# Cosine attention followed by a highway layer: half-batch loads and norms, a power on GpSimd, first quads turned on TensorE, a new planned order

## The chip, the cores and the metric

The kernel runs on one core of a Trainium2 chip. The metric is the time of one execution on the device in microseconds (us); smaller is better. Before the change two executions took 439.52 and 444.78 us, a median of 442.15 us. The profiled execution has a span of 442.0 us; all times inside the kernel below are from that one.

## The reference

There are 8 batches, 12 heads, 448 positions and a head size of 64. Queries and keys are divided by their own norms, the scores are scaled by 1/tau = 10, and a softmax over the keys weighs the values. The heads are then put side by side to rows of 768, and a highway layer is applied to the 3584 rows.

```python
q_n = q / (np.linalg.norm(q, axis=-1, keepdims=True) + 1e-06)
k_n = k / (np.linalg.norm(k, axis=-1, keepdims=True) + 1e-06)
scores = np.matmul(q_n, k_n.transpose(0, 1, 3, 2)) / tau
attn = np.exp(scores - np.max(scores, axis=-1, keepdims=True))
attn = attn / (np.sum(attn, axis=-1, keepdims=True) + 1e-09)
x = np.matmul(attn, v)                    # then (batch, position, head x 64)
H = np.maximum(x @ w_h, 0.0)
T = 1.0 / (1.0 + np.exp(-(x @ w_t + b_t)))
out = T * H + (1.0 - T) * x
```

Since normalised rows have scores of at most 10 in size, both kernels leave out the subtraction of the maximum.

## The kernel before

**Units of work.** Four heads of one batch are a *quad* (24 in all, three a batch), two heads are a *pair* (48), and 128 rows of the highway layer are a *tile* (28). A batch gives three tiles of its own, and the 64 positions that are left over in each batch are joined for two batches into a fourth tile (`xl`), so two batches make seven tiles.

**A quad on its way.** GpSimd (POOL) issues the loads of queries and keys (L260), which turn fp32 into fp16 on the way, into one of five `raw` buffers. VectorE (DVE) squares them (L275), folds the squares twice (L282, L289) and sums them (L294). When the three quads of a batch are there, eight small VectorE operations on 84 values a partition (`newton`, L307 to L313) give the inverse norms `rs`; in batch 0 this is done for each quad by itself. GpSimd multiplies queries and keys with them into one of two `qkn` buffers (L361, L365, L369; 15 rows a quad, since one row of the queries is kept twice). Two DMA transposes issued by SyncE (L387) then turn `qkn` into one of three `qkT` buffers. VectorE copies the values into `vp` with a further column for the sum of the weights (L397, L398, L399).

**A pair on its way.** TensorE (PE) makes the scores in four steps (L422, L425), ScalarE (ACT) takes the exponential of each step (L438, L440), PE multiplies with the values in 32 small matmuls (L463), and VectorE divides by the sum (L471, L473, L477) into `xb` and, for the left-over positions, `st`.

**A tile on its way.** When the six pairs of a batch are done, SyncE moves the left-over rows (L496) and turns the three blocks of `xb` (L514) into `xT`. PE multiplies each with both weights, in two halves each (L525; the bias is one more matmul, L528). VectorE takes relu minus x (L539), ScalarE the tanh (L546), VectorE adds 1 to it, multiplies and makes the last sum (L557, L558, L559), and SyncE stores the rows (L575). The kernel carries x/2 in place of x (the value of the sum column is 2), so that the tanh needs no scale.

**What sets the order.** All of this is a list of operations with an engine, a cost in ns, a due step, the operations it depends on, and the buffers that it takes and drops. `Planner.plan` runs the list once at build time: each engine takes, of the operations that are ready by the planned times, the one with the lowest due step. The result is written out as a fixed order for each engine. On the chip every engine works through its own order and waits at an operation whose inputs or buffers are not there, however much work stands ready behind it. The planner's costs are therefore no times of the chip, but they decide which operation stands before which. PSUM has three shared banks (`pb`) for the attention result and the halves of the highway layer, two double banks for the scores and one bank for their last step.

Of the kernel before, what the change touches and what calls it, by code (L numbers as in the profile page):

```python
# [7 lines left out]

# [6 lines left out]


class Op:
    __slots__ = ("eng", "dur", "fn", "deps", "step", "takes", "drops", "mode",
                 "land", "start", "end", "left", "users", "seq", "name", "after", "issued")

    def __init__(self, name, eng, dur, step, fn, deps=(), takes=(), drops=(), mode=None, land=None, after=()):
        self.name, self.eng, self.dur, self.step, self.fn = name, eng, dur, step, fn
        self.deps = [d for d in deps if d is not None]
        self.takes, self.drops, self.mode, self.land = list(takes), list(drops), mode, land
        self.start = self.end = None
        self.users = []
        self.after = [d for d in after if d is not None]


class Ring:  # L30


    def __init__(self, bufs):
        self.free = list(range(len(bufs)))
        self.bufs = bufs
        self.where = {}
        self.users = {}
# [5 lines left out]
class Planner:  # L43


    SYNC = 90
    SWITCH = 93
    DMA_FIX = 1900
    GBPS = 300.0
# [4 lines left out]
    def add(self, *a, **k):  # L54
        op = Op(*a, **k)
        op.seq = len(self.ops)
        self.ops.append(op)
        return op

    def plan(self):  # L60
        ready = {e: [] for e in ("PE", "ACT", "DVE", "POOL", "SP")}
# [4 lines left out]
        for op in self.ops:  # L66
            if op.left == 0:
                ready[op.eng].append((0.0, op))
        free = {e: 0.0 for e in ready}
        dma_free = 0.0  # L70
        mode = None
        now = 0.0
        pend = []
        order = []
        n = len(self.ops)
        while len(order) < n:
# [8 lines left out]
            for e in ready:  # L85
# [3 lines left out]
                for t, op in ready[e]:  # L89
                    if t > now:  # L90
                        continue
                    need = {}
# [4 lines left out]
                    key = op.step  # L97
                    if e == "PE" and mode is not None and op.mode == mode and mode == "q":
# [6 lines left out]
                ready[e].remove((t, op))  # L105
                for ring, key in op.takes:
                    ring.where[key] = ring.free.pop(0)
                dur = op.dur
# [5 lines left out]
                free[e] = op.issued = now + dur  # L114
                end = now + dur
                if op.land is not None:
                    begin = max(end, dma_free)
                    dma_free = begin + op.land / self.GBPS
                    end = dma_free + self.DMA_FIX
                op.end = end  # L120
                for ring, key in op.drops:
                    pend.append((end + self.SYNC, ring, ring.where[key]))
                for u in op.users:
                    u.left -= 1
                    if u.left == 0:
                        r = max([d.end + (self.SYNC if (d.eng != u.eng or d.land is not None) else 0) for d in u.deps]
                                + [d.issued for d in u.after])
                        ready[u.eng].append((r, u))
# [6 lines left out]
            nxt += [t for t, _, _ in pend if t > now]  # L135
            if not nxt:
# [3 lines left out]
        self.span = max(o.end for o in self.ops)  # L140
        return order


@with_exitstack
def kernel(
# [20 lines left out]
    pool = ctx.enter_context(tc.tile_pool(name="sb", bufs=1))  # L166
    psum = ctx.enter_context(tc.tile_pool(name="ps", bufs=1, space=bass.MemoryType.PSUM))

    def ring(name, n, shape, dt, space=None):
        return Ring([(space or pool).tile(shape, dt, name=f"{name}{i}", tag=f"{name}{i}") for i in range(n)])  # L170

    w_sb = [pool.tile([128, CC, DM], FP16, name=n, tag=n) for n in ("w_h", "w_t")]
    brow = pool.tile([128, DM], FP16, name="brow", tag="brow")
    ones = pool.tile([128, 128], FP16, name="ones", tag="ones")
    braw = pool.tile([1, DM], FP32, name="braw", tag="braw")

    raw_r = ring("raw", 5, [128, 2, 2, 7, D], FP16)
    sq_r = ring("sq", 2, [128, 28, D], FP16)
# [446 lines left out]
```

## Time and profile before

| What | us | Share of the 442.0 us |
|---|---|---|
| PE busy | 273.3 | 62% |
| DVE busy | 258.7 | 59% |
| ACT busy | 170.1 | 38% |
| POOL busy | 147.0 | 33% |
| DMA: q1, what SyncE issued, of 16 engines | | 51.6% |
| DMA: q0, what GpSimd issued, of 16 engines | | 21.1% |
| Mean granted TensorE clock | | 0.837 of full |

A group of instructions is named by its line, its engine and what it writes and reads (out<-in). A wait is time in which an engine stood still, put down to whatever released it last. "SPq" is the queue of SyncE, on which DMAs are issued. Busy times of PE are those of pipelined matmuls, so two matmuls that overlap count once. In a timeline, the first number is the start, the second how long the row lasted; "x6" is a row of six instructions merged.

Two rows of the page give the prices that matter most here: an exponential of 896 elements takes 921 ns (L438, 144 times, 126.2 us in all), and a product of 448 elements on GpSimd takes 992 ns in the mean (L365, 48 times, 46.5 us).

### The profile page before, as it was taken

The page shows a single profiled execution, that of the slowest core. Times are in us where ns is not written, and L with a number is a line of the kernel's source. Part 1 is how long each engine was busy: PE and PEld are TensorE (multiplying, and loading weights), DVE is VectorE, ACT ScalarE, POOL GpSimd, SP SyncE. Part 2 cuts the span into 40 slices and gives each one's busy share as a digit, 9 for nine tenths or more (in the row PEclk, how much of TensorE's full clock was granted, in tenths as well). Part 3 has the DMA queues.
Part 4 walks back from the last instruction along what each step waited for, and adds up shares of the span by engine and source line. Part 5 has one row for each costly group of instructions (what it writes and reads, how often), then busy time and mean ns, then how long its engine had stood idle before and what let it go on. Part 6 is the DMA issues. An engine that isn't in the chain of part 4 may idle for free.

```text
span 442.0 us, 6960 instructions
## 1 busy us (share of the span) xinstructions
PE 273.3 (62%) x2648; PEld 149.6 (34%) x2648; DVE 258.7 (59%) x556; ACT 170.1 (38%) x249; POOL 147.0 (33%) x207
## 2 busy tenths in 40 slices
PE   0014382768519595298509596496709696698494
PEld 0003151343304353154304344243405344255252
DVE  2893254285915859159914868549823968365154
ACT  1022361336405263066504373073704373178021
POOL 5657005620366005650176005460085005430000
PEclk9999556796959889599957988799958988899798
DMA  8699932996099930999179951999269941872413
GB/s 171 106 186 188 180 52 48 180 162 148 2 162 177 190 78 25 186 207 177 36 109 171 200 75 38 149 204 199 59 84 184 172 117 36 153 116 55 99 42 101
DMA packets 111234, 55.50 MB, mean 126 GB/s; under 512 B 81505, under 2 KB 107617, under 8 KB 111202
## 3 DMA queue, kind: packets, MB, share of 16 engines
q1 hardware_dynamic: 96578, 41.70, 51.6%
q0 software_dynamic: 14624, 13.37, 21.1%
q8 instruction: 20, 0.33, 0.3%
q14 instruction: 12, 0.10, 0.1%
HBM read 39.32 MB, written 11.01 MB: 114 GB/s over the span
## 4 chain that ended last, share of the span: by engine, by line
DMA 31%; PE 25%; DVE 20%; POOL 9%; SPq 7%; issue 5%; ACT 2%; POOLq 0%; DVEq 0%; ACTq 0%
DMA qkT<-qkn 24%; PE pb L525 16%; DMA xT<-xb 5%; PE pb L463 4%; PE sc L422 4%; POOL qkn L365 3%; POOL raw L260 3%; DVE xb L473 3%; SPq L387 2%; SPq L514 2%; SPq L496 2%; DVE sq L275 2%; POOL qkn L369 2%; DVE o L559 1%; DMA out_dram<-o 1%
## 5 line engine op out<-in xcount | busy, mean ns | idle before, releaser
L438 ACT ACTIVATE ex<-sc 128x896 f16<-128x896 f32 x144 | 126.2, 921 | 109.7 <-PE sc L422 109.5
L525 PE MATMUL pb<-w_h,xT 128*128 128x384 f16 x336 | 80.1, 393 | 81.0 <-DMA xT<-xb 74.4
L525 PEld LDWEIGHTS <-xT 128*128 128x128 f16 x672 | 68.3, 109 | 152.2 <-DMA xT<-xb 75.9
L361 POOL TENSOR_TENSOR qkn<-raw,rs 128x128 f16<-128x128 f16 x48 | 20.2, 439 | 242.8 <-DVE rd L471 183.8
L422 PE MATMUL sc<-qkT 64*128 64x448 f16 x288 | 51.2, 397 | 65.3 <-DMA qkT<-qkn 60.2
L546 ACT ACTIVATE t<-pb 128x384 f16<-128x384 f32 x56 | 27.7, 494 | 155.8 <-PE pb L528 155.6
L525 PE MATMUL pb<-w_t,xT 128*128 128x384 f16 x336 | 70.9, 352 | 3.6 <-DVE d L539 3.0
L463 PE MATMUL pb<-vp,ex 128*128 128x65 f16 x1536 | 64.0, 200 | 12.6 <-DVE st L477 6.5
L463 PEld LDWEIGHTS <-ex 128*128 128x128 f16 x1536 | 58.8, 102 | 24.8 <-issue 14.7
L539 DVE SCALAR_TENSOR_TENSOR d<-pb,xb 128x384 f16<-128x384 f32 x48 | 25.3, 551 | 67.8 <-PE pb L525 67.8
L365 POOL TENSOR_TENSOR qkn<-raw,rs 128x448 f16<-128x448 f16 x48 | 46.5, 992 | 0.2
L369 POOL TENSOR_TENSOR qkn<-raw,rs 128x384 f16<-128x384 f16 x48 | 44.2, 940 | 0.0
L422 PEld LDWEIGHTS <-qkT 64*128 64x128 f16 x288 | 11.9, 96 | 91.2 <-DMA qkT<-qkn 62.5
L557 DVE TENSOR_SCALAR t<-t 128x768 f16<-128x768 f16 x28 | 18.7, 669 | 37.1 <-ACT t L546 37.0
L471 DVE RECIPROCAL rd<-pb 128x7 f32<-128x7 f32 x48 | 9.7, 201 | 47.3 <-PE pb L463 47.0
L275 DVE TENSOR_TENSOR sq<-raw 128x1792 f16<-128x1792 f16 x24 | 26.0, 1084 | 6.7 <-DMA raw<-in_k_dram 6.5
L473 DVE TENSOR_TENSOR xb<-pb,rd 128x384 f16<-128x384 f32 x48 | 26.7, 557 | 1.6
L440 ACT ACTIVATE ex<-sl 128x448 f16<-128x448 f32 x48 | 26.4, 550 | 0.0
L559 DVE SCALAR_TENSOR_TENSOR o<-xb,d 128x768 f32<-128x768 f16 x24 | 24.6, 1026 | 0.8
L558 DVE TENSOR_TENSOR d<-t,d 128x768 f16<-128x768 f16 x28 | 23.8, 849 | 1.0
L425 PE MATMUL sl<-qkT 64*64 64x448 f16 x96 | 19.9, 411 | 0.0
L528 PE MATMUL pb<-brow,ones 128*128 128x384 f16 x56 | 18.6, 332 | 0.0
(37 smaller groups left out, 169.9 us busy)
## 6 DMA issues: line engine op xcount, KB each, us to landing
out_dram<-o SPq DMA_DIRECT2D x48, 192.0 KB, 2.8
vraw<-in_v_dram SPq DMA_DIRECT2D x8, 768.0 KB, 9.6
raw<-in_q_dram POOLq DMA_DIRECT2D x24, 224.0 KB, 9.2
raw<-in_k_dram POOLq DMA_DIRECT2D x24, 224.0 KB, 9.8
vraw<-in_v_dram SPq DMA_DIRECT2D x8, 576.0 KB, 6.6
vraw<-in_v_dram SPq DMA_DIRECT2D x8, 192.0 KB, 10.9
out_dram<-o SPq DMA_DIRECT2D x4, 384.0 KB, 3.2
w_h<-in_moe_w_h_dram POOLq DMA_DIRECT2D x1, 1152.0 KB, 10.7
```

Of the source, the lines that this page charges most:

```text
L275: nc.vector.tensor_mul(sq_r[k_][:, :, :], r, r)
L365: nc.gpsimd.tensor_mul(qkn[:, 1:8, g, :], raw[:, 0, g], rs[:, 0, g].unsqueeze(2).to_broadcast([128, 7, D]))
L369: nc.gpsimd.tensor_mul(qkn[:, 8:14, g, :].rearrange("p (j i) d -> p i j d", i=2), raw[:, 1, g, 0:6, :].rearrange("p (i j) d -> p i j d", i=2),
L422: nc.tensor.matmul(sc_r[n, j][:, g, 0:S], lhsT=T[:, 512 + 128 * j : 640 + 128 * j], rhs=rhs, start=True, stop=True)
L438: nc.scalar.activation(o, sc_r[n, j][:, :, 0:S], AF.Exp, scale=inv_tau)
L440: nc.scalar.activation(ex[:, 3136 : 3136 + S], sl_r[n][:, 0:S], AF.Exp, scale=inv_tau)
L463: nc.tensor.matmul(u[:, s * 65 : s * 65 + 65], lhsT=l, rhs=r, start=(m == 0), stop=(m == len(ms) - 1))
L473: nc.vector.tensor_tensor(out=xo, in0=u[:, 0:6, 0:D].rearrange("p (g i) e -> p g i e", g=2), in1=rd[:, 0:6].rearrange("p (g i) -> p g i", ...
L525: nc.tensor.matmul(pt[:, 0:MH], lhsT=xT[:, c, :], rhs=w_sb[w][:, c, ms], start=(c == 0), stop=(w == 0 and c == CC - 1))
L539: nc.vector.scalar_tensor_tensor(out=d_r[m][:, h], in0=pb_r[m, w, h][:, 0:MH], scalar=0.0, in1=xsrc()[:, ms], op0=ALU.max, op1=ALU.subtract)
L546: nc.scalar.activation(t_r[m][:, h], pb_r[m, w, h][:, 0:MH], AF.Tanh)
L559: nc.vector.scalar_tensor_tensor(out=o_r[m][:, :], in0=xsrc(), scalar=2.0, in1=d, op0=ALU.mult, op1=ALU.add)
```

## The change

The loads come in half batches, each into one of three `raw` buffers of a whole batch, batch 0 still in three parts. Squares, folds and sums work on the same halves. In batches 0 and 1 the inverse norms are still Newton steps, for each part; in the other six batches one GpSimd operation raises the 84 sums of squares to the power -0.5. `qkn` gets a third buffer, and its rows are 14 in place of 15. The first two quads (all of batch 0 but its last third) are not turned by DMA: their products are shared out between GpSimd and VectorE, PE turns them against an identity into PSUM, and ScalarE or VectorE copies them to `qkT`. The values are copied by ScalarE or VectorE and their last row is masked on GpSimd in one operation a batch; `vp` now holds a batch. x is carried whole: the tanh is scaled by 0.5, the gate is (t+1)/2, by VectorE or GpSimd, and the last sum, d + x, can be made by GpSimd too. The weights are loaded in halves. Many planner costs are new, an operation may be given to whichever of two engines is free first, and loads are planned only while the planned DMA backlog is small.

It is meant to have norms and transposes ready earlier, to lift small work off VectorE, and to start the first scores without waiting for DMA.

In the order that the new planner gives, 15 of the 28 last sums, 9 of the 28 gates and all 8 masked copies stand on GpSimd; 15 of the 24 copies of values and the 4 copies of turned quads on ScalarE; 10 of the 12 products of the first two quads on VectorE. On PE the finished batch's first tile comes after the scores and attention of the next batch's first one or two pairs, but for the boundary of batches 1 and 2; before, it came ahead of the next batch's scores at each boundary.

The core of the diff:

```diff
-    SYNC = 90
-    SWITCH = 93
-    DMA_FIX = 1900
-    GBPS = 300.0
+    SYNC = 70
+    SWITCH = 95
+    LATE = 1900
+    DEPTH = 2500
...
+                    if op.dma is not None and op.dma[1] == "load" and dma_free > now + self.DEPTH:
+                        continue
...
-    raw_r = ring("raw", 5, [128, 2, 2, 7, D], FP16)
...
-    qkn_r = ring("qkn", 2, [128, 15, 2, D], FP16)
...
+    raw_r = ring("raw", 3, [128, 2, 6, 7, D], FP16)
...
+    qkn_r = ring("qkn", 3, [128, 14, 2, D], FP16)
+    qkT_r = ring("qkT", 3, [128, 2, 14, 64], FP16)
...
+    vp_r = ring("vp", 2, [128, NH, 4, 66], FP16)
...
-    xb_r = ring("xb", 3, [128, 3, DM], FP16)
+    xb_r = ring("xb", 2, [128, 3, DM], FP16)
...
+        return lambda op: nc.gpsimd.dma_start(w_sb[i][:, 3 * h : 3 * h + 3, :], src[:, 3 * h : 3 * h + 3, :])
+
+    w_ops = {(i, h): add(f"w{i}{h}", ("POOL", 890), (-1.8, -1.6, -1.4, -1.2)[2 * i + h], w_load(i, h), dma=(3350, "load"))
+             for i in range(2) for h in range(2)}
...
+        return lambda op: nc.gpsimd.dma_start(raw_r[b][:, t, lo:hi], src[:, 6 * b + lo : 6 * b + hi, :])
...
-            lq = add(f"lq{k_}", "POOL", 1000, s0 - 9, mk_load(k_, 0), takes=[(raw_r, k_)], land=128 * 896 * 4,
-                     after=[qT_op.get((k_ - 3, 1))])
-            lk = add(f"lk{k_}", "POOL", 1000, s0 - 9, mk_load(k_, 1), after=[lq], land=128 * 896 * 4)
...
-            o = add(f"nw{b}", "DVE", 8 * 225, steps(b * NQ) - 4.5, newton(b, 0, 84), deps=[red_ops[b * NQ + 2]],
-                    takes=[(rs_r, b)], drops=[(n2_r, b)])
-            norm_ops[b] = [o, o, o]
...
+        parts = [(0, 2), (2, 4), (4, 6)] if b == 0 else [(0, 3), (3, 6)]
+        for lo, hi in parts:
+            for t in range(2):
+                o = add(f"l{'qk'[t]}{b}_{lo}", ("POOL", 730), 6 * b - 9 + lo * (0.3 if b == 1 else 1), mk_load(b, t, lo, hi),
+                        takes=[(raw_r, b)] if lo == 0 and t == 0 else [], dma=(700 * (hi - lo), "load"))
+                if not (lo == 0 and t == 0):
+                    o.after.append(ld[b, 0, 0])
+                for i in range(lo, hi):
...
+        def power(b):
+            def fn(op):
+                nc.gpsimd.tensor_tensor(out=rs_r[b][:, :, :], in0=n2_r[b][:, :, :],
+                                        in1=half[:, :].unsqueeze(2).to_broadcast([128, 2, 42]), op=ALU.pow)
+            return fn
+
+        groups = parts if b < 2 else [(0, 6)]
+        prev = None
+        for lo, hi in groups:
+            first, last = lo == 0, hi == 6
+            kw = dict(deps=[reds[parts.index((lo, hi))]] if b < 2 else reds, after=[prev],
+                      takes=[(rs_r, b)] if first else [], drops=[(n2_r, b)] if last else [])
+            if b < 2:
+                o = add(f"nw{b}_{lo}", ("DVE", 8 * (195 + 14 * (hi - lo) * 1.042)), 6 * b + lo - 4.5, newton(b, lo, hi), **kw)
+            else:
+                o = add(f"nw{b}_{lo}", ("POOL", 2500), 6 * b + lo - 4.5, power(b), **kw)
...
+        for w, n in enumerate((128, 64, 448, 384, 384, 384)):
+            engs = {"POOL": (pool(n), 0.0)}
+            if k_ < NPE:
+                engs["DVE"] = (dve(n), 0.0)
+            o = add(f"nm{k_}_{w}", engs, s0 - 3.5, nm_fn(k_, b, qd, w), deps=[rs_op[b, 2 * qd], rs_op[b, 2 * qd + 1]], after=nms[:1],
+                    takes=[(qkn_r, k_)] if w == 0 else [])
+            nms.append(o)
+        if lastq:
+            nms[-1].drops += [(raw_r, b), (rs_r, b)]
...
+        if k_ < NPE:
+            cps = []
+            for t in range(2):
+                def pt_fn(op, k_=k_, t=t):
+                    ps = pb_r["tr", k_, t][:, 0:448].bitcast(FP16)
+                    for s in range(7):
+                        nc.tensor.transpose(ps[:, 128 * s : 128 * s + 128],
+                                            qkn_r[k_][:, 7 * t + s].rearrange("p g d -> p (g d)"), ident[:, :])
+
+                need = nms[1:4] if t == 0 else [nms[0]] + nms[4:]
+                pt = add(f"pt{k_}_{t}", ("PE", 7 * 55), s0 - 2.5, pt_fn, deps=need + [i_id], takes=[(pb_r, ("tr", k_, t))],
+                         mode="f")
...
+                def cp_fn(op, k_=k_, t=t):
+                    ps = pb_r["tr", k_, t][:, 0:448].bitcast(FP16).rearrange("p (s a l) -> p s a l", s=7, a=2)
+                    dst = qkT_r[k_][:, :, 7 * t : 7 * t + 7, :].rearrange("p a s l -> p s a l")
+                    if op.eng == "ACT":
+                        nc.scalar.copy(dst, ps)
...
+                cp = add(f"cp{k_}_{t}", {"ACT": (act(896), 0.0), "DVE": (dve(896, 2), 0.0)}, s0 - 2.5, cp_fn, deps=[pt], after=cps,
+                         takes=[(qkT_r, k_)] if t == 0 else [], drops=[(pb_r, ("tr", k_, t))])
...
+            nc.gpsimd.tensor_mul(vp_r[b][:, :, 3, 0:D], vraw_r[b][:, :, 3, :], mask[:, :].unsqueeze(2).to_broadcast([128, NH, D]))
+
+        vlo = add(f"vl{b}", ("POOL", pool(768)), 6 * b - 1.5, vl_fn, deps=vl[b] + [ini_m] + ini_vp, takes=[(vp_r, b)])
+        prev = vlo
...
+            o = add(f"vc{b}_{qd}", {"ACT": (act(768), 0.0), "DVE": (dve(768, 2), 1.5)}, 6 * b + 2 * qd - 1.0, vc_fn,
+                    deps=vl[b], after=[prev], drops=[(vraw_r, b)] if qd == NQ - 1 else [])
...
+        def g_fn(op, m=m):
+            t = t_r[m][:, :, :].rearrange("p h m -> p (h m)")
+            eng = {"POOL": nc.gpsimd, "DVE": nc.vector}[op.eng]
+            eng.tensor_scalar(out=t, in0=t, scalar1=1.0, scalar2=0.5, op0=ALU.add, op1=ALU.mult)
...
-            nc.vector.tensor_scalar(out=t, in0=t, scalar1=1.0, scalar2=None, op0=ALU.add)
...
+        g1 = add(f"g{m}", {"DVE": (380, 0.0), "POOL": (900, 1.5)}, s0 + 1.8, g_fn, deps=el)
+        gg = add(f"h{m}", ("DVE", 590), s0 + 1.8, h_fn, deps=[g1], drops=[(t_r, m)])
...
+            eng.tensor_add(o_r[m][:, :], d, xsrc())
+
+        oo = add(f"o{m}", {"POOL": (pool(768), 0.0), "DVE": (dve(768), 1.5)}, s0 + 1.9, o_fn, deps=[gg], takes=[(o_r, m)],
...
-            nc.vector.scalar_tensor_tensor(out=o_r[m][:, :], in0=xsrc(), scalar=2.0, in1=d, op0=ALU.mult, op1=ALU.add)
```

## The prediction

> **What bounds the kernel now.** I read the page's slices first, then the waits in order of their total, then the timelines around one batch boundary, then the busy time by stretch. In the slices no engine is full for long:
>
> ```profile
> PE   0014382768519595298509596496709696698494
> POOL 5657005620366005650176005460085005430000
> DMA  8699932996099930999179951999269941872413
> ```
>
> One digit is 11 us. PE and the DMA engines alternate: DMA stands at 9 while PE is in the middle of its range and at 0 to 3 where PE is at 9, and POOL works in bursts with empty slices between. That is a chain that hands work round, once a batch. The list of waits (total us, times, longest us) names the hand-overs:
>
> ```profile
> POOL qkn L361 <- DVE rd L471: 183.8, 7, 28.9
> ACT ex L438 <- PE sc L422: 109.5, 38, 28.1
> PE pb L525 <- DMA xT<-xb: 74.4, 8, 13.7
> PE sc L422 <- DMA qkT<-qkn: 60.2, 10, 29.5
> POOL qkn L361 <- DMA qkT<-qkn: 46.7, 8, 7.3
> ```
>
> POOL sits 26 us, seven times, before the first normalisation of a batch. L471 is only the neighbour in VectorE's order; what it needs is the Newton step (L307 to L313). VectorE's timeline before batch 2 (start us, length us) shows why that is late:
>
> ```profile
> 105.21 0.22 DVE L399 CAST vp<-vraw 64x128 f16<-64x128 f32 x1
> 109.86 0.20 DVE L471 RECIPROCAL rd<-pb 128x7 f32<-128x7 f32 x1 [4.43 <-PE pb L463]
> ...
> 110.77 1.08 DVE L275 TENSOR_TENSOR sq<-raw 128x1792 f16<-128x1792 f16 x1
> ...
> 116.94 0.24 DVE L313 SCALAR_TENSOR_TENSOR rs<-nt,rs 128x84 f32<-128x84 f32 x1
> ```
>
> The squares of the third quad stand behind the division of the batch before, which waits for PE. So batch 2's norms end at 117.2, when batch 1's attention ends too. PE's timeline at that point:
>
> ```profile
> 117.02 1.09 PE L463 MATMUL pb<-vp,ex 128*128 128x65 f16 x29 [0.23 <-ACT ex L440]
> 130.73 3.83 PE L525 MATMUL pb<-w_h,xT 128*128 128x384 f16 x12 [12.62 <-DMA xT<-xb]
> ...
> 135.62 0.55 PE L422 MATMUL sc<-qkT 64*128 64x448 f16 x4
> ```
>
> PE has nothing for 12.6 us: in its order the highway tile of the finished batch stands before the next scores, and both sets of transposes start together. The stretches show it from the DMA side (PE, PEld, DVE, ACT and POOL busy, clock, DMA share, GB/s):
>
> ```profile
> 105.00:122.00 17.00, 11.74 (x166) 6.95 (x163) 11.44 (x31) 10.60 (x16) 4.67 (x6) 0.90 0.07 20
> 126.00:158.00 32.00, 22.11 (x159) 10.77 (x159) 15.76 (x27) 10.88 (x16) 9.65 (x14) 0.77 1.12 180
> 158.00:174.00 16.00, 13.89 (x187) 8.22 (x185) 13.36 (x33) 10.77 (x16) 2.80 (x5) 1.00 0.14 41
> ```
>
> For 16 us DMA does a tenth, for 32 us it is crowded (packets overlap, so a share may exceed 1; 90 to 102 us reaches 1.33). What PE can do when fed stands in a stretch near the end:
>
> ```profile
> 389.18:398.04 8.86, 8.86 (x109) 5.14 (x106) 5.92 (x13) 6.59 (x11) 1.87 (x2) 1.00 0.58 113
> ```
>
> Those 8.86 us are two head pairs and one tile, without a gap.
>
> **Three parts of the span.** Batch 0's last attention matmul ends at 68.9 us, batch 7's at 410.4, the kernel at 442.0: start 68.9, seven batches of 48.8, tail 31.6. In the dense stretch a tile's four halves take 1.25+1.15+1.08+0.99 = 4.47 us from start to next start, so a pair costs (8.86-4.47)/2 = 2.2, and a batch of 6 pairs and 3.5 tiles 6x2.2+3.5x4.47 = 28.8 us of PE. DMA: the share of 0.81 over a batch times 48.8 is 39.5 us of engine time; at the 1.33 seen when crowded that is 29.7 us. So about 30 us a batch is the floor of both, and 18.8 us a batch are lost in the hand-overs.
>
> **What the Trainium skill says.** "SBUF — State Buffer", section "SBUF: two separate sides": VectorE and GpSimd share one port pair as an exclusive lock, taken by VectorE operations in a two-port mode or with two SBUF inputs. The trace agrees: from 118.1 to 120.4 two L365 take 2.30 us beside an L558 of 1.17, alone they take 1.84 and 0.56. "GPSIMD Engine Reference", section 3.1, gives some 2.6 cycles at 1.2 GHz an element for two inputs, 0.97 us for 448; L365 has a median of 0.947. No page and no row prices a power there. "DMA: Bandwidth & Descriptors", section "Issuing engines are not separate DMA queues": all queues share the 16 engines; landing of qkT ranges from 3.6 to 16.3 us here.
>
> **The change, part by part.**
>
> Loads and norms. The raw ring grows from 5 quads (1.7 batches) to 3 batches, and loads come by half batch: same bytes, 34 issues in place of 48, POOL 14x0.74 = 10 us less. More important is the order that results on VectorE. Before, the Newton step of each of batches 2 to 7 has only two divisions of pairs between it and the batch's first pair. After, the last square of batches 3, 4, 5, 6 and 7 has 6, 6, 6, 8 and 7 of them; only batch 2 stays at two. On PE the scores of the next one or two pairs now stand before the finished batch's first tile at six of seven boundaries; at batch 1 to 2 tile 3 still goes first. So the waits of 74.4 us lose their cause at six places; the last, 5.3 us, stays in the tail.
>
> Power on GpSimd. Six batches lose 8 VectorE operations of 0.20 to 0.25 (1.95 us) and gain one operation on 84 elements. L365 against L369 gives (947-829)/64 = 1.84 ns an element, 0.12 fixed: 0.27 us is the low end. High end: the change books 2.5 us; as nothing shows it I allow 10. I take 2.5, 15 us in all. Queued behind it are the batch's normalisations, for which the transposes wait; with 6 pairs of lead that hides, except in batch 2.
>
> VectorE. Out go 40 of 80 Newton operations, 18-8 = 10 us, 15 of 24 value copies to ScalarE with all 48 short ones (0.40+0.36 us each) to GpSimd, 27 us, and 15 of 28 final sums (1.03), 15 us: with 4 us of normalisations back, 259 falls to about 210, 26 a batch. ScalarE gains 15 copies of 768 and 4 of 896, 0.8 to 0.92 by L438: 16 us, 170+16 is 23 a batch. Both are below 30.
>
> POOL. In come 15 sums and 8 masked copies of 768 elements, 23x(0.12+768x0.00184 = 1.53) = 35, nine gates at about 0.9 = 8, powers 15; out 10 for issues and 8 for two quads: 147+40 = 187, 23 a batch, 26 with the stretch seen under the lock. Below 30, but the masked copy, gate and sum wait on DMA, ScalarE and VectorE, and normalisations stand behind them.
>
> Transposes. Rows 15 to 14 and 24 to 22 quads take 14% off qkT. In steady state only the 1/15 counts, under 1 us a batch.
>
> Start. First scores at 29.5 now: normalised at 20.1, landed 9.4 later. After: Newton ends 15.3, six normalisations over two engines 2 to 2.5 us, 14 PE transposes about 1.5, copies about 1 to 2: 20 to 21. Quad 1: its squares follow on VectorE, 4.3 us, its products 2.3, then as before: 26.5. Pairs take 3.3 us on ScalarE (3x0.92+0.55): quads 0 and 1 end near 33. Quad 2 is normalised by 32.6 and must pass the crowded DMA (batch 1, weights): 8 us between 3.6 and 16.3, so 41, plus two pairs: batch 0 ends near 47 (43 to 56) in place of 68.9.
>
> Tail: the same four tiles, the last sum still on VectorE; 31.6 stays.
>
> Sum: of the 18.8 us lost a batch I leave 8, for in-order VectorE (a half batch's square, 1.08x1.5 = 1.6 us, now blocks a PSUM drain), the one unfilled boundary, and crowded DMA. 47+7x38+31.6 = 344.6, say 345.
>
> **Rivals.** Crowded DMA stays the limit: PE asks now for transposes while loads run, and each lands 10 us late, as in the first 60 us. For it speaks landing of 5.6 median under load; against it the 16 idle us a batch. Batch 43: 47+301+31.6 = 380. POOL becomes the bound, power at 10 us or normalisations stuck behind a sum: 23+8 to 23x1.3+10 = 40, with waits 46: 401. Slower: four POOL waits a batch on the tanh, product, sum chain, each of 6.6 us (the longest wait of L557), block POOL: 26+4x6.6 = 52.4; with a start as before, since the same queue feeds it, 68.9+367+31.6 = 467. Against it: six pairs of lead (some 27 us at the dense pace) absorb most.
>
> **How the numbers follow.** Main 0.63 at 345; DMA 0.25 at 380; POOL 0.07 at 401; slower 0.05 at 467. The range takes a batch of 34 with a start of 44 (314) up to 390, past the DMA case. Faster by over 2% (below 433): 0.92, within 0.03, slower 0.05.
>
> **What would show it.** Right: POOL's 183.8 wait gone or small, PE's wait on xT under 25 us, first scores near 20, batch 0 over near 47, DMA without empty slices, L377 under 3 us. Wrong: PE still waiting on qkT each batch with DMA above 1.2, or normalisations that start late behind L650, L637 or L477.

## The result, and the profile after

The changed kernel takes 390.75 us (median of 390.39 and 391.11) beside 442.15 us before: a ratio of 0.884, with a 95% interval of 0.861 to 0.907. It is faster, as forecast, but by 51 us and not by 97; the measured time lies just above the range of 314 to 390. Some executions of a program are some per cent longer than its others, at a lower granted clock: the times here and below are medians of all executions, the ratios count the faster ones alone.

The part of the page that cuts the span into 40 slices (9.7 us each now):

```profile
PE   0157467991669819399371697836997996898593
POOL 7346773339999996579984998799729992012031
DMA  7993999999476299995799999944986069311724
```

The slices of PE are still uneven, and DMA still has holes (slices of 0 to 4), but POOL, which before worked in bursts, is full for long stretches from slice 10 (at 87 us) to slice 33 (ends at 321 us). The page's chain of work that ended last, by engine and by line:

```profile
PE 30%; POOL 29%; DMA 15%; issue 10%; DVE 9%; SPq 4%; ACT 2%; POOLq 1%; DVEq 0%; ACTq 0%
PE pb L608 18%; POOL rs L377 14%; PE pb L545 6%; POOL qkn L420 4%; DMA qkT<-qkn 4%; PE sc L508 4%; DMA raw<-in_k_dram 4%; DMA vraw<-in_v_dram 3%; DMA xT<-xb 3%; POOL qkn L417 2%; POOL qkn L415 2%; DMA out_dram<-o 2%; DVE sq L337 2%; POOL raw L290 2%; POOL t L637 2%
```

The second costliest line of that chain is L377, the power. Its own row in the trace (number, min/median/max in ns, first and last start in us):

```profile
L377 POOL TENSOR_TENSOR rs<-n,half x6: 13731/13752/14073, 89.5 to 292.9; 128x84 f32<-128x84 f32 x6
```

It takes 13.75 us, where the forecast had 2.5 and allowed 10 at most. From the list of waits (total us, times, longest us):

```profile
POOL o L650 <- DVE d L642: 54.7, 9, 18.0
PE pb L608 <- DMA xT<-xb: 42.3, 7, 10.9
DVE sq L337 <- DMA raw<-in_k_dram: 40.1, 10, 12.1
PE pb L608 <- DVE st L559: 16.6, 2, 10.0
PE sc L508 <- DMA qkT<-qkn: 15.9, 4, 5.8
```

POOL's wait of 183.8 us before the first normalisation is gone, and PE's wait on qkT fell from 60.2 to 15.9. But PE still waits 42.3 us on xT, and VectorE now waits 40.1 us on raw data (6.5 before). GpSimd's timeline at the end of batch 1, which is over at 89.3 (start us, length us):

```profile
88.07 0.80 POOL L290 DMA_DIRECT2D raw<-in_k_dram  x1
89.46 13.77 POOL L377 TENSOR_TENSOR rs<-n,half 128x84 f32<-128x84 f32 x1 [0.59 <-DVE n L356]
103.30 0.40 POOL L411 TENSOR_TENSOR qkn<-raw,rs 128x128 f16<-128x128 f16 x1
...
113.32 1.61 POOL L420 TENSOR_TENSOR qkn<-raw,rs 128x384 f16<-128x384 f16 x2
114.89 13.73 POOL L377 TENSOR_TENSOR rs<-n,half 128x84 f32<-128x84 f32 x1
```

Batch 2's power stands in front of its three quads' normalisations, and batch 3's follows at once: both lie inside batch 2. The busy time by stretch, from one batch's last attention matmul to the next one's, batches 2 to 5 (PE, PEld, DVE, ACT and POOL busy, clock, DMA share, GB/s):

```profile
89.30:152.30 63.00, 37.52 (x343) 20.07 (x343) 29.11 (x54) 23.89 (x35) 62.34 (x46) 0.76 0.75 129
152.30:198.70 46.40, 33.09 (x327) 18.01 (x326) 23.82 (x40) 22.57 (x33) 36.10 (x27) 0.85 0.94 161
198.70:246.60 47.90, 33.43 (x338) 19.49 (x339) 29.92 (x47) 21.75 (x32) 38.24 (x31) 0.82 1.23 155
246.60:289.30 42.70, 31.97 (x331) 17.52 (x331) 24.17 (x41) 22.45 (x34) 33.30 (x25) 0.88 0.83 149
```

In batch 2 POOL is busy for 62.34 of 63.00 us: there it is full, though its mean over the span is 67%. In the next three it is at 78 to 80%.

The parts of the span: the start 54.2 us (68.9 before), batches 1 to 7 in 35.1, 62.9, 46.5, 47.9, 42.7, 34.3 and 34.9 (49.2, 54.4, 45.1, 55.7, 46.0, 53.2, 38.0 before), the tail 30.8 (31.6).

### The profile page after: what moved, and what is told of

Same layout as the page of the kernel before. It is cut to its first block, busy times and chain, and to the rows that moved or that the text cites. A ratio compares the mean times of both kernels' runs of the same rounds, so it can differ in the third digit from the quotient of the medians.

```text
span 389.3 us, 6889 instructions
## 1 busy us (share of the span) xinstructions
PE 270.4 (69%) x2676; PEld 152.5 (39%) x2676; DVE 206.0 (53%) x403; ACT 184.3 (47%) x268; POOL 261.7 (67%) x225
## 4 chain that ended last, share of the span: by engine, by line
PE 30%; POOL 29%; DMA 15%; issue 10%; DVE 9%; SPq 4%; ACT 2%; POOLq 1%; DVEq 0%; ACTq 0%
PE pb L608 18%; POOL rs L377 14%; PE pb L545 6%; POOL qkn L420 4%; DMA qkT<-qkn 4%; PE sc L508 4%; DMA raw<-in_k_dram 4%; DMA vraw<-in_v_dram 3%; DMA xT<-xb 3%; POOL qkn L417 2%; POOL qkn L415 2%; DMA out_dram<-o 2%; DVE sq L337 2%; POOL raw L290 2%; POOL t L637 2%
## 5 line engine op out<-in xcount | busy, mean ns | idle before, releaser
L608 PE MATMUL pb<-w_h,xT 128*128 128x384 f16 x336 | 77.1, 387 | 52.3 <-DMA xT<-xb 42.3
L377 POOL TENSOR_TENSOR rs<-n,half 128x84 f32<-128x84 f32 x6 | 82.8, 13804 | 11.7 <-DVE n L356 9.2
L508 PE MATMUL sc<-qkT 64*128 64x448 f16 x288 | 51.8, 392 | 27.5 <-DMA qkT<-qkn 15.9
L545 PE MATMUL pb<-vp,ex 128*128 128x65 f16 x1536 | 62.5, 199 | 5.7 <-DVE d L619 2.0
L650 POOL TENSOR_TENSOR o<-d,xb 128x768 f32<-128x768 f16 x14 | 23.6, 1685 | 61.6 <-DVE d L642 54.7
L337 DVE TENSOR_TENSOR sq<-raw 128x2688 f16<-128x2688 f16 (+1 forms) x17 | 30.1, 1771 | 40.1 <-DMA raw<-in_k_dram 40.1
L619 DVE SCALAR_TENSOR_TENSOR d<-pb,xb 128x384 f16<-128x384 f32 x48 | 26.2, 554 | 35.8 <-PE pb L608 35.7
L420 POOL TENSOR_TENSOR qkn<-raw,rs 128x384 f16<-128x384 f16 x45 | 39.9, 902 | 0.1
L637 DVE TENSOR_SCALAR t<-t 128x768 f16<-128x768 f16 x19 | 8.4, 443 | 49.0 <-ACT t L626 49.0
L415 POOL TENSOR_TENSOR qkn<-raw,rs 128x448 f16<-128x448 f16 x23 | 22.6, 982 | 7.5 <-DVE rs L372 7.5
L642 DVE TENSOR_TENSOR d<-t,d 128x768 f16<-128x768 f16 x28 | 19.6, 699 | 14.8 <-POOL t L637 14.1
L417 POOL TENSOR_TENSOR qkn<-raw,rs 128x384 f16<-128x384 f16 x22 | 24.2, 1098 | 0.0
L553 DVE RECIPROCAL rd<-pb 128x7 f32<-128x7 f32 x48 | 9.6, 199 | 27.4 <-PE pb L545 27.3
L477 POOL TENSOR_TENSOR vp<-vraw,mask 128x768 f16<-128x768 f32 x8 | 12.8, 1599 | 12.2 <-DMA vraw<-in_v_dram 8.6
```

The source lines that it names most:

```text
L337: nc.vector.tensor_mul(sq_r[key][:, 0:n].rearrange("p (t s) d -> p t (s d)", t=2), r, r)
L377: nc.gpsimd.tensor_tensor(out=rs_r[b][:, :, :], in0=n2_r[b][:, :, :], in1=half[:, :].unsqueeze(2).to_broadcast([128, 2, 42]), op=ALU.pow)
L415: eng.tensor_mul(qkn[:, 0:7, 0, :], raw[:, 0, 0], rs[:, 0, 0].unsqueeze(2).to_broadcast([128, 7, D]))
L417: eng.tensor_mul(qkn[:, 1:7, 1, :], raw[:, 0, 1, 0:6], rs[:, 0, 1, 0:6].unsqueeze(2).to_broadcast([128, 6, D]))
L420: eng.tensor_mul(qkn[:, 7:13, g, :].rearrange("p (j i) d -> p i j d", i=2), raw[:, 1, g, 0:6, :].rearrange("p (i j) d -> p i j d", i=2), r ...
L508: nc.tensor.matmul(sc_r[n, j][:, g, 0:S], lhsT=T[:, 448 + 128 * j : 576 + 128 * j], rhs=rhs, start=True, stop=True)
```

## The experiments

My theory after this profile: the power is the whole of the miss, and the rest of the forecast holds. The rivals: the order itself costs (crowded DMA, normalisations behind sums, gates and copies), or the power was only planned with a wrong duration. Each ratio is to the kernel before, which ran again beside each group of runs (medians of 439 to 442 us), with its 95% interval.

| Run | us | Ratio to before |
|---|---|---|
| changed kernel | 390.8 | 0.884 (0.861 to 0.907) |
| multiplication in place of the power | 342.4 | 0.777 (0.772 to 0.782) |
| Newton on VectorE, same order | 347.7 | 0.791 (0.787 to 0.796) |
| Newton, planned as such | 344.1 | 0.781 (0.777 to 0.785) |
| power, planned with 13.8 us | 391.1 | 0.889 (0.884 to 0.894) |
| power and half a power more | 432.9 | 0.987 (0.980 to 0.995) |
| power by half batch, planned with 7.05 us | 352.3 | 0.800 (0.794 to 0.806) |
| power split in place | 393.2 | 0.895 (0.888 to 0.901) |
| power, two loads put in front of it | 386.8 | 0.879 (0.870 to 0.888) |
| power, gates and sums on VectorE | 383.8 | 0.874 (0.869 to 0.879) |
| power in batch 2 alone, Newton in the others | 355.1 (347.1 to 362.6) | none |
| Newton, all last sums on VectorE | 358.2 | 0.815 (0.808 to 0.822) |
| Newton, no quads on TensorE | 372.9 | 0.849 (0.843 to 0.855) |
| Newton, three quads on TensorE | 346.0 | 0.784 (0.778 to 0.791) |
| Newton, batch 2 in halves, four sums held | 354.9 | 0.809 (0.802 to 0.816) |
| Newton, batch 2 in halves | 355.5 | 0.802 (0.792 to 0.811) |
| Newton, landing planned with 4.0 us | 350.6 | 0.796 (0.790 to 0.801) |

### Is it the power?

```diff
-                                        in1=half[:, :].unsqueeze(2).to_broadcast([128, 2, 42]), op=ALU.pow)
+                                        in1=half[:, :].unsqueeze(2).to_broadcast([128, 2, 42]), op=ALU.mult)
```

> The power of L377 becomes a multiplication on the same engine, with the same operands, at the same place in the same order; the inverse norms are then not the reference's, so one operation's cost is left out and nothing else is changed. Theory (the 13.8 us of each power on GpSimd is what the forecast missed: six of them, each in front of the normalisations of its batch): L377 falls below 1 us and the time to 340 us (332 to 350), batches 1 to 5 to 36 to 42 us each. Rival (the order itself: crowded DMA, or normalisations queued behind sums, gates and copies): the time stays at 375 us or above, and PE's waits on qkT and xT grow.

Measured 342.4 us. This kernel leaves the power out, so its inverse norms are not those of the reference. The row of L377 in this run:

```profile
L377 POOL TENSOR_TENSOR rs<-n,half x6: 315/325/642, 89.7 to 247.9; 128x84 f32<-128x84 f32 x6
```

The same operands, the same form, 0.33 us in place of 13.75, and 48 us are gone: the time that was forecast. Six of them took 80.8 us more on GpSimd (82.8 busy less six of 0.33), of which 48 came out at the end. By batch, 62.9 became 43.9, then 46.5, 47.9 and 42.7 became 41.0, 36.5 and 33.2 (36 to 42 was expected). Batches 2 and 3 in this run:

```profile
89.70:133.60 43.90, 31.65 (x341) 18.17 (x343) 31.37 (x51) 23.50 (x35) 41.18 (x46) 0.88 1.09 175
133.60:174.60 41.00, 29.82 (x327) 17.12 (x329) 23.89 (x40) 22.48 (x33) 23.03 (x29) 0.88 1.19 201
```

The rival that blamed the order falls. The Newton step put back on VectorE, without and with a plan that knows of it:

```diff
-                o = add(f"nw{b}_{lo}", ("POOL", 2500), 6 * b + lo - 4.5, power(b), **kw)
+                o = add(f"nw{b}_{lo}", ("POOL", 2500), 6 * b + lo - 4.5, newton(b, 0, 6), **kw)
```

> The plan is made as before, with the power booked at 2.5 us on GpSimd, but what is written at that place is the Newton step on VectorE, 8 operations of 0.2 to 0.25 us; all other instructions keep their order. Theory (the power on GpSimd is the cause): within 6 us of the run with the multiplication, about 342 us, since 1.95 us of VectorE in each of six batches is hidden. Rival (order and DMA): 375 us or above. A third way: VectorE's step lies behind divisions that wait for PE, as in the kernel before, and it comes out between 350 and 370.

```diff
-                o = add(f"nw{b}_{lo}", ("POOL", 2500), 6 * b + lo - 4.5, power(b), **kw)
+                o = add(f"nw{b}_{lo}", ("DVE", 8 * (195 + 84 * 1.042)), 6 * b + lo - 4.5, newton(b, 0, 6), **kw)
```

> The Newton step on VectorE in all batches, and booked there with its own cost, so the plan is free to change: more sums and gates go to GpSimd. Theory (power is the cause): 335 to 345 us, at or below the run with Newton in the old place. Rival (order and DMA): 370 us or above. If it is slower than Newton in the old place by over 5 us, VectorE's load or GpSimd's sums set the pace next.

Measured 347.7 and 344.1 us. So the eight VectorE operations a batch cost 2 to 5 us in all where the power that replaced them cost 48. The planned one leaves nothing out and is faster than both kernels, 344.1 us beside 390.8 and 440.

### Its duration, and what more of it costs

```diff
                                         in1=half[:, :].unsqueeze(2).to_broadcast([128, 2, 42]), op=ALU.pow)
+                nc.gpsimd.tensor_tensor(out=rs_r[b][:, :, 0:21], in0=n2_r[b][:, :, 0:21],
+                                        in1=half[:, :].unsqueeze(2).to_broadcast([128, 2, 21]), op=ALU.pow)
```

> The changed kernel, with a second power on GpSimd behind each of the six, over half of the 84 columns (the result of those is written twice, the same). Two questions. What sets the duration: if it goes with the elements, the second operation takes 6.9 us; if most of the 13.8 us is fixed, about 13. And what a further us of power costs: theory (it lies in front of the normalisations, mostly on the path; 6 x 13.5 us cost 390.8 - 342.4 = 48 us, 0.6 us for each us): 6 x 6.9 x 0.6 = 25 us more, or nearer 41 as the lead is used up by now: 416 to 432. Rival (the time of the changed kernel comes from its order): within 10 us of 390.8.

Measured 432.9 us. The second operation's row:

```profile
L379 POOL TENSOR_TENSOR rs<-n,half x6: 7053/7055/7061, 103.4 to 341.6; 128x42 f32<-128x42 f32 x6
```

(13.751 - 7.055)/42 = 0.159 us an element and 0.36 us fixed, on the line through these two sizes: nearly all of it goes with the elements. The added 42.3 us (6 x 7.06) cost 42.1 us, which is all of it, to within the 10 us or so that the interval of the changed kernel leaves. The first 80.8 us cost 48, so it seems that what slack there was is used up.

### Only planned with a wrong duration?

```diff
-                o = add(f"nw{b}_{lo}", ("POOL", 2500), 6 * b + lo - 4.5, power(b), **kw)
+                o = add(f"nw{b}_{lo}", ("POOL", 13800), 6 * b + lo - 4.5, power(b), **kw)
```

> The power stays on GpSimd, but the planner is told 13.8 us for it in place of 2.5, so the order changes: fewer sums and gates go to GpSimd, and tiles are put where the power would leave PE idle. Theory (83 us of GpSimd time, in front of each batch's normalisations, can't be planned away): 370 us or above. Rival (it was only planned with a wrong duration, and a right one hides it in the six pairs of lead): about 345 us.

Measured 391.1 us: the true cost alone brings nothing. Its busy time by batch (2 to 5) shows what its plan made:

```profile
89.50:135.80 46.30, 34.49 (x344) 19.29 (x344) 26.71 (x49) 22.40 (x34) 46.14 (x27) 0.85 0.68 134
135.80:180.20 44.40, 32.17 (x320) 17.60 (x318) 22.44 (x41) 20.83 (x30) 20.49 (x25) 0.77 0.96 166
180.20:230.90 50.70, 35.81 (x344) 20.70 (x344) 32.70 (x51) 21.58 (x32) 50.52 (x32) 0.87 0.63 124
230.90:272.90 42.00, 30.25 (x318) 16.75 (x318) 26.05 (x43) 20.87 (x30) 19.14 (x19) 0.84 0.91 159
```

POOL is busy 46.14 of 46.30 us in one batch and 20.49 of 44.40 in the next, then again 50.52 of 50.70 and 19.14 of 42.00: two powers fall into one batch and at most 3.6 us of one into the next. POOL is full half of the time and waits the other half.

Then the power cut in two operations of 42 columns, one behind each half batch, and planned with 7.05 us each:

```diff
-        groups = parts if b < 2 else [(0, 6)]
+        groups = parts
...
-                o = add(f"nw{b}_{lo}", ("POOL", 2500), 6 * b + lo - 4.5, power(b), **kw)
+                o = add(f"nw{b}_{lo}", ("POOL", 7050), 6 * b + lo - 4.5, power(b, lo, hi), **kw)
```

> The changed kernel with each of the six powers cut in two of 42 columns, 7.05 us each, one behind each half batch, and planned with that duration. The same 83 us on GpSimd, but the first half's normalisations wait for 7 us in place of 13.8, and the first step comes a half batch earlier. If what costs is the delay in front of the normalisations, 355 to 370 us. If it is GpSimd's time, which the loads, copies, sums and normalisations of the same in-order engine can't get back, 380 to 395.

Measured 352.3 us, just under the lower of the two ranges, with GpSimd nearly as busy as in the changed kernel (252.5 us beside 261.7). Its busy time by batch, 2 to 5:

```profile
89.40:137.10 47.70, 33.48 (x341) 18.32 (x341) 34.39 (x48) 23.92 (x35) 40.37 (x32) 0.82 0.97 167
137.10:177.30 40.20, 31.72 (x331) 17.30 (x331) 31.50 (x46) 22.86 (x35) 36.13 (x27) 0.92 0.90 152
177.30:214.50 37.20, 31.89 (x336) 18.37 (x337) 25.55 (x44) 21.24 (x32) 35.64 (x27) 0.91 1.08 177
214.50:250.50 36.00, 30.44 (x332) 16.80 (x331) 23.04 (x43) 22.07 (x33) 35.68 (x25) 0.91 0.95 166
```

POOL's work lies evenly now, 36 to 40 us a batch, and in the last two batches shown it alone fills them (35.64 of 37.20, 35.68 of 36.00). So the same powers cost 39 us less in this run. It changes three things at once: the powers are spread; each starts half a batch earlier, so that batch 2's first products begin at 86.7 us in place of 103.3; and the new plan leaves GpSimd 5 last sums and 6 gates fewer. My expectation had named the delay in front of the normalisations as the reason. The next run shortens that delay alone.

### By which way does it cost?

```diff
-                nc.gpsimd.tensor_tensor(out=rs_r[b][:, :, :], in0=n2_r[b][:, :, :],
-                                        in1=half[:, :].unsqueeze(2).to_broadcast([128, 2, 42]), op=ALU.pow)
+                half_power(b, slice(0, 21))
...
+                if what == 0 and b > 1 and qd == 1:
+                    half_power(b, slice(21, 42))
                 if what == 0:
```

> The changed kernel, its plan unchanged, with each power cut in two of 42 columns: the first half at the power's place, the second behind the normalisation of the batch's first quad, which needs only the first half. GpSimd's work is the same to 0.4 us a batch; only the first quad's products come 6.7 us earlier, and the long operation is broken once. If what costs is the lateness of a batch's own first transposes, 352 to 375 us. If it is GpSimd's time taken from everything queued on it, sums, gates and later products, within 6 us of 390.8.

Measured 393.2 us: a batch's first products 7 us earlier (at 96.2 us in batch 2) bring nothing in the old plan. So a shorter delay in front of the first quad is not enough; the run before has the products of batch 2's three quads earlier by 17, 7 and 5 us, this one the first by 7 and the two others later by 3, so it doesn't settle what an earlier start of all three is worth. In batch 2 (89.5 to 155.8 us) POOL is busy for 65.87 of 66.30 us, full as in the changed kernel. Next, what stands behind the power:

```diff
     order = P.plan()
+    for p in [op for op in order if op.name[:2] == "nw" and op.eng == "POOL"]:
+        i = order.index(p)
+        nxt = [op for op in order[i:] if op.eng == "POOL" and op.dma is not None and op.dma[1] == "load"][:2]
+        for op in nxt:
+            order.remove(op)
+            order.insert(order.index(p), op)
```

> The changed kernel with its power, its plan unchanged, but the next two half-batch loads behind each power in GpSimd's order are put in front of it (buffers are free by then). The power's own place in front of the normalisations stays. In the changed kernel VectorE waits 40.1 us for raw data (11.5 with the multiplication), and DMA has empty slices, since the loads stand behind the power. If the later batches lose their time by that queue, 365 to 378 us and VectorE's wait on raw below 20. If they lose it because their own normalisations, or gates and sums, are late behind the power, within 6 us of 390.8.

I had this from a chain in the changed kernel. PE's, and VectorE's, timeline:

```profile
134.12 0.55 PE L508 MATMUL sc<-qkT 64*128 64x448 f16 x4
144.68 1.76 PE L608 MATMUL pb<-w_h,xT 128*128 128x384 f16 x5 [10.01 <-DVE st L559]
```

```profile
141.64 2.15 DVE L337 TENSOR_TENSOR sq<-raw 128x2688 f16<-128x2688 f16 x1 [12.12 <-DMA raw<-in_k_dram]
143.71 0.19 DVE L553 RECIPROCAL rd<-pb 128x7 f32<-128x7 f32 x1
143.94 0.56 DVE L555 TENSOR_TENSOR xb<-pb,rd 128x384 f16<-128x384 f32 x1
144.41 0.21 DVE L559 TENSOR_TENSOR st<-pb,rd 128x64 f16<-128x64 f32 x1
```

The load was issued at 136.0, behind the power; VectorE stood at its square, with a division behind it, and PE wanted the PSUM bank that the division reads. That chain is real, and with the loads in front VectorE's wait on raw fell to 10.6 us. But the time is 386.8: batch 2 became shorter by 9.2 us, batch 3 longer by 4.1, PE's wait on xT grew from 42.3 to 53.5. POOL is again busy for 53.50 of the 53.70 us of batch 2. The longest wait in view was not the one that mattered.

```diff
-            eng = {"POOL": nc.gpsimd, "DVE": nc.vector}[op.eng]
+            eng = nc.vector
             eng.tensor_scalar(out=t, in0=t, scalar1=1.0, scalar2=0.5, op0=ALU.add, op1=ALU.mult)
...
-            eng = {"POOL": nc.gpsimd, "DVE": nc.vector}[op.eng]
+            eng = nc.vector
             eng.tensor_add(o_r[m][:, :], d, xsrc())
```

> The changed kernel with its power and its order, but the gates and last sums that stood on GpSimd are made by VectorE, at the same place in the order (9 gates and 15 sums, 18 to 24 us more on VectorE, 33 us less on GpSimd). If what costs is that gates and sums stand behind the power, and the highway layer's buffers and PSUM with them, 360 to 378 us. If it is the batch's own normalisations, which still stand behind it, 385 us or above.

Measured 383.8 us, 7 less: 33 us of gates and sums off GpSimd, and a small part of the loss with them. Neither expectation was met. By batch, batch 3 fell from 46.5 to 40.6 us, where the multiplication has 41.0; what batch 5 won (10.3 us), batch 6 lost but for 1.5. Batch 2 stayed at 63.1 us although POOL was busy for only 57.00 of them, so a full POOL is not by itself what makes that batch long: PE again stood for 11.29 us, for a PSUM bank whose division stood behind a square that waited for raw data.

```diff
-                o = add(f"nw{b}_{lo}", ("POOL", 2500), 6 * b + lo - 4.5, power(b), **kw)
+                o = add(f"nw{b}_{lo}", ("POOL", 2500), 6 * b + lo - 4.5, power(b) if b == 2 else newton(b, 0, 6), **kw)
```

> The changed kernel in its own order, the power left on GpSimd in batch 2 alone, where two pairs of lead stand in front of it; in the five others the Newton step is written at the same place, as in the run that had it in all six (347.7 us). If batch 2's power costs its whole duration on the path and no more, 347.7 + 13.5 = 361 us, and the five others, which have six pairs and more of lead, cost the remaining 30 us. If it costs 19, as the difference between the two profiles in that batch suggests (62.9 and 43.9 us), 367. If the lead of two pairs hides it, below 352.

Inconclusive: its four executions spread from 347.1 to 362.6 us, so that one power costs anything from nothing to 15. In the profile (the shortest execution) batch 2 took 52.2 us: 4.7 more than with Newton in all batches, and 10.7 less than in the changed kernel, where batch 3's power lies in batch 2 too.

### The other parts of the change

All on the planned Newton (344.1 us). The last sums:

```diff
-        oo = add(f"o{m}", {"POOL": (pool(768), 0.0), "DVE": (dve(768), 1.5)}, s0 + 1.9, o_fn, deps=[gg], takes=[(o_r, m)],
+        oo = add(f"o{m}", {"DVE": (dve(768), 0.0)}, s0 + 1.9, o_fn, deps=[gg], takes=[(o_r, m)],
```

> Newton on VectorE, and all 28 last sums on VectorE too: the edit that moved sums to GpSimd is undone, the planner makes a new order. If that edit carries part of the gain, VectorE (65% busy, then 70%) delays the divisions and the time goes from 344 to 350 to 360 us. If it costs, because loads and normalisations wait in GpSimd's order behind sums that wait up to 12 us for their product, it falls to 332 to 340. In between: it doesn't matter here.

Measured 358.2 us, as the first case said: with its new plan, the sums on GpSimd are worth some 13 to 14 us. The quads on TensorE, none and three in place of two:

```diff
-    NPE = 2
+    NPE = 0
```

> Newton on VectorE, and the first two quads transposed by DMA like all others: the edit that turns them on TensorE is undone, and their normalisations go to GpSimd alone. My reading of the start: first scores near 29 in place of 20.6, as in the kernel before, and batch 0 over at 60 to 64 in place of 54.6, so 350 to 354 us. Rival (quad 2's transposes, landed near 46, set the end of batch 0 whatever quads 0 and 1 do): batch 0 still over near 55, and 344 us.

Measured 372.9 us. The edit is worth 29 us and not the 6 to 10 that I read into the start: batch 0 is over at 57.7 us, only 3 later, but batch 1 takes 48.0 in place of 35.4. One of its waits shows where to look:

```profile
PE sc L508 <- DMA qkT<-qkn: 46.2, 8, 27.3
```

27.3 us of the 46.2 are the first scores of the kernel; 19 are left for later transposes, where the run with two quads on TensorE has 4.6 in all. The order is another one as well (21 of the last sums on GpSimd in place of 17), so the 29 us belong to the edit with its new plan, and the transposes' part is not shown by itself.

```diff
-    NPE = 2
+    NPE = 3
```

> Newton planned on VectorE, and a third quad (batch 0's last) normalised and transposed as the first two are, on TensorE. In the changed kernel batch 0 is over at 54.2 us where 47 was forecast: quad 2 is normalised on GpSimd until 38.6 (32.6 was forecast), its transposes land at 45.8, two pairs follow. Theory (that chain is the whole of the difference): batch 0 over at 47 to 50, and the rest as in the run with two quads, so 337 to 341 us. Rival (VectorE, which takes a share of the products, is late anyway, or what is won is lost in batch 1 to loads and transposes): batch 0 over at 52 or later, or batch 1 longer by as much, 344 us.

Measured 346.0 us. Batch 0 is over at 51.1, 3.5 earlier: half of the miss of 7 in the start was quad 2's way over GpSimd and DMA. What was won there, and 8 us in batch 2, was given back in batches 3 to 6 (154 us in place of 141).

### A better order?

Three runs on the planned Newton, whose batch 2 took 50.4 us.

```diff
-        groups = parts if b < 2 else [(0, 6)]
+        groups = parts if b < 3 else [(0, 6)]
...
-        oo = add(f"o{m}", {"POOL": (pool(768), 0.0), "DVE": (dve(768), 1.5)}, s0 + 1.9, o_fn, deps=[gg], takes=[(o_r, m)],
+        oo = add(f"o{m}", {"DVE": (dve(768), 0.0)} if m < 4 else {"POOL": (pool(768), 0.0), "DVE": (dve(768), 1.5)}, s0 + 1.9, o_fn, deps=[gg], takes=[(o_r, m)],
```

> Newton on VectorE, for batch 2 in two steps, one behind each half batch, and the last sums of the first four tiles kept on VectorE, so that no load waits behind them on GpSimd. In the run with the planned Newton batch 2 took 50.4 us where the other batches took 29 to 37, since its norms were done only at 93 us, with batch 1 over at 90. If that is the reason, batch 2 falls to 36 to 42 and the time to 330 to 337 us. If DMA (share 1.17 there) is the reason, batch 2 stays near 50 and the time at 344.

The first of these lines without the second:

> Newton planned on VectorE, for batch 2 in two steps, one behind each half batch; the last sums stay free to go to GpSimd. The run with this and with the sums of four tiles held on VectorE had batch 2 in 41.9 us in place of 50.4, but batches 1, 3, 4 and 5 longer by 3.8 to 5.7 us each. If those were lost to the sums on VectorE: batch 2 near 42, the others near those of the planned Newton, 334 to 340 us. If they were lost to the order of the tiles that an earlier batch 2 brings: 350 to 355 us again.

```diff
-    LATE = 1900
+    LATE = 4000
```

> Newton planned on VectorE, and the planner told 4.0 us in place of 1.9 from a transfer's end to its landing, since transposes land 7 us and more after their issue in the trace. If the order's wrong belief about landing costs time (tiles put in PE's order before their transposes are in: 31 us of waits on xT), 334 to 341 us; if those waits come from crowded DMA whatever the order, 344 to 350.

Measured 354.9, 355.5 and 350.6 us, none better. In the first, batch 2 fell to 41.9 as expected, and batches 1, 3, 4 and 5 grew by 4 to 6 each. Without the held sums the second, whose executions spread from 350.4 to 358.1 us, is no better, but in its profile the loss lies elsewhere: batches 1, 3 and 5 are back at 35.8, 38.0 and 38.2 us, and batch 2 takes 48.6 and batch 4 44.8. So neither reading of its expectation holds as it stands, and which of the moves in the order costs stays open.

## Why the prediction was wrong

- **The power.** The step that failed is "as nothing shows it I allow 10. I take 2.5, 15 us in all". It is 13.75 us, 82.8 in all; even the high end was passed. The low end came from products of 384 and 448 elements, the high end from nothing that was measured. That alone is the miss: with a multiplication at its place the time is 342.4, with Newton planned 344.1, where 344.6 was worked out.
- **"With 6 pairs of lead that hides, except in batch 2".** Half wrong. Of the 80.8 us that the powers added, 48 came out in the time. Lead counts pairs on PE; it didn't count GpSimd's own queue, where batch 3's power moved up into batch 2 and filled that engine for 62.34 of 63.00 us. Batches 3 to 5 lost 5 to 11 us each with POOL at 78 to 80%.
- **The sum 47 + 7x38 + 31.6.** Without the power (the run with the multiplication): 54.4 + 252.8 + 31.1. The start was 7 too low, the batches 13 too high (36.1 each), the tail right. So 345 was near for a kernel without the power partly by luck: two errors met.
- **The start.** First scores at 20.55, as forecast. "Quad 2 is normalised by 32.6": it was 38.6, since its norms came at 32.5 and three of GpSimd's products then took 2.1, 1.2 and 1.2 in place of 0.8 each. Landing 45.8 (forecast 41), then 8.4 us for two pairs (6).
- **Waits on xT "under 25 us", L377 "under 3 us", DMA "without empty slices".** All three failed. With Newton planned the first is still 30.9 us, and why is not shown; the slices of DMA have no 0 then. POOL's wait of 183.8 went, as said. Neither sign of being wrong came as named: the normalisations started late, but behind L377 itself.
- **VectorE and ScalarE.** 206.0 and 184.3 us busy, 210 and 186 forecast. POOL: 261.7; 187 forecast; less what the powers took beyond 15 us, 194.
- **The rivals.** "POOL becomes the bound, power at 10 us", 401 us, had a chance of 0.07 and is the one that was right in kind: POOL is full in batch 2, though not over the span. The measured time lies as near to crowded DMA, 380, which had 0.25 and was not the cause: with the power gone the same DMA work fitted into 342 us.

What stays open: how the powers cost time in batches 3 to 5, where POOL isn't full. Its loads, its gates and sums, and its first products were each taken out of the power's way, for -4, -7 and +2 us. Powers in halves, spread and started earlier in a new plan, gave 39. That spread load on the in-order engine is the reason is what the busy times by batch suggest; which hand-over it frees, and what the earlier start alone is worth, isn't shown. And not all of the loss is waiting: in batches 2 and 3 PE was busy for 37.52 + 33.09 = 70.6 us at a granted clock of 0.76 and 0.85, with the multiplication for 31.65 + 29.82 = 61.5 us at 0.88 (670 and 668 matmuls). So of the 24.5 us that these two batches lost, up to 9 are matmuls that took longer; how much of that lay on the path, and why the clock was lower, isn't shown.

## What to carry to other kernels

An operation that no row of the trace shows has no upper bound from a neighbour of the same form: either the range must be wide enough for a factor of forty (0.33 to 13.75 us here), or the operation is measured alone first. A mean busy share of 67% can hide an engine that is full for a whole batch and waits in the next; read busy time stage by stage, above all for an engine that works through a fixed order and is given new work. And a wait in the list is no promise: taking away 30 us of VectorE's wait on raw data returned 4 us.

## What the runs showed of the hardware that was not expected

- A power on GpSimd takes 13.75 us for 84 elements a partition and 7.06 for 42, some 0.159 us an element between the two, while a multiplication with the same operands takes 0.33 for 84.
- The long power does not hold VectorE's squares up. The Trainium skill, "SBUF — State Buffer", section "SBUF: two separate sides", says of a VectorE operation with two SBUF inputs and a GpSimd operation that reads SBUF that whichever starts first has the shared port pair for its whole instruction, and the other blocks. While the power of 13.77 us ran from 89.46, two squares of 2688 elements on VectorE took what the median of this line is (1.56 us), and so did two more under later powers (1.56 us each, at 214.31 and 249.76):

```profile
91.81 1.55 DVE L337 TENSOR_TENSOR sq<-raw 128x2688 f16<-128x2688 f16 x1
...
98.16 1.56 DVE L337 TENSOR_TENSOR sq<-raw 128x2688 f16<-128x2688 f16 x1 [1.61 <-DMA raw<-in_k_dram]
```

  Beside GpSimd's products the same square took 2.15 us (at 141.64) and 3.02 (at 191.69). So a power doesn't keep VectorE out for its whole instruction here; the measurement decides, and whether or how long a power holds the pair isn't shown.
